# A fused recurrence, gated MLP and expert layer: TensorE's order planned with its instruction supply, one more group inverted in 32x32 blocks, an untaken branch moved to GpSimd, rows stored in four parts

## The chip, the cores and the metric

The kernel runs on one core of one Trainium2 chip. The metric is device microseconds of one launch. The kernel before took 984.58 us (median of 3 runs, 982.29 to 986.92).

## What is computed

Three stages follow one another, cut here to their core:

```python
# 1. a recurrence over S=768 steps, for B=4 batches and H=8 heads, state 40x40
y[t]  = r[t] @ state
Sa    = state @ a[t]
state = state * w[t] - outer(Sa, b[t]) + outer(v[t], k[t])
# 2. a gated MLP on x = y with the heads side by side (320 columns)
h = relu(x @ w_in); u, v = h[:, :512], h[:, 512:]
x = (u * (w_spatial @ layernorm(v) + b_spatial)) @ w_out
# 3. eight experts: a row goes to its argmax expert, or keeps the expert of the row
#    before it (a sequential choice along the 768 rows of a batch)
out = p[e] * (relu(x @ w1[e]) @ w2[e])
```

## The kernel before, in words

**Attention** (`attention`, from L158; 0 to 474 us) turns the recurrence into chunks of 64 steps. There are 12 chunks for each of 4 batches, 48 in all, numbered q = 0 to 47 with the batches interleaved; each handles all 8 heads as 4 pairs in the two halves of the partitions. Inside a chunk the steps depend on each other through a 64x64 triangular matrix per head, which has to be inverted. The chunks are inverted in seven groups (q 0 to 3, then 4 to 11, 12 to 19, 20 to 27, 28 to 35, 36 to 43, 44 to 47). A letter per group in `KEYS['inv']` (L57) says how. "b": VectorE inverts the 32x32 diagonal blocks by 31 pairs of a product and a subtraction (`prod` L321, `diff` L324), and TensorE joins two blocks to 64x64 (`c1` L391, `c2` L399). "c": VectorE inverts 16x16 blocks by 15 shorter pairs (`prod16` L332, `diff16` L335), and TensorE joins them first to 32x32, with two more sets of tiny products for every two chunks (`gA` L366, `pA` L376 and L379) and a VectorE correction between them (`gAc` L368). An fp32 product of these is two passes, and every pass is a weight load and a matmul, so that `pA` for two chunks is 192 instructions. Before the change the letters are `ccbcbcb`: four groups of 16x16, three of 32x32.

Per chunk there is also preparation: decay products by scans (`stF` L258, L262), scalings of k, b and a (`stK` L268, `stB` L273, on VectorE or GpSimd as the planner finds them free), their products (`stQ` L280, `stT` L298) and copies and masks on ScalarE and GpSimd. Then comes the chain of the chunk itself: `s`, `z`, `w`, `t`, `y` on TensorE (L434, L443 with L415, L452 and L453, L462, L470 and L471), with a copy or product on ScalarE or VectorE behind each (L436, L446, L456, L465 and L466, L476 and L478).

The order of all of this is not written by hand: `plan` (L58) simulates the engines on the host from a duration per operation (the numbers in the `add(...)` calls from L510 on), priorities computed from `KEYS`, and dependencies, and gives the list in which the instructions are issued. When TensorE has nothing ready, `fill` (L96) puts in dummy matmuls (`heat` L229, `tied` L239), which are there to keep TensorE's clock up. The planner keeps its own count of how busy TensorE has been (`cols`, `hw`, `th`, `hp`) and slows TensorE's durations when that is low. Loading and checking of the decays (`guard`) and some weight preparation of the MLP are fitted in among it, at priorities `gp` and `pp`.

**The branch.** The chunked form needs decays in a range; `guard` counts those outside. Behind attention all engines load the flag and branch (L1522, L1523) over `general` (L626), a loop of 12 times 64 steps with nine VectorE instructions a step. With these inputs it is never entered.

**The middle** (`middle`; to about 700 us) is the MLP; TensorE goes on there with `vprod` (L874), whose first operands VectorE splits at the end of attention (L816).

**The tail** (`tail`, to 754 us) finishes the last batch: output products (`outp`, copied to `xr` by L967 and L968), the gate's logits, the routing (`Q["begin"]` to `Q["enter"]`, mostly tiny VectorE operations: `begin` L1058 to L1075, `probs` L1078 to L1081, `rows` L1088 to L1091, `back` L1098 to L1100, `places` and `pick` L1105 to L1123, `enter` L1126), the storing of the rows for the experts' gathers (`store` L1130, on SP's queue), the slot tables (`slots`, `first`, `slots2`, L1135 to L1211), and for the first expert's weights, loaded by `prefetch` in five pieces, the split into two fp32r halves: `split` (L1237) casts a piece on ScalarE (L1240) and subtracts on VectorE or GpSimd (L1241, L1242). Before:

```python
Q["rows"](0); G.outp(0, xr); G.logits(LG, 1, ident, M.lt)
M.split(0, 0, G.nc.gpsimd)
Q["begin"](1); G.outp(1, xr); R["enter"](1); Q["rows"](1)
M.split(0, 1, G.nc.gpsimd)
G.outp(2, xr); Q["back"](); G.outp(3, xr, mid=Q["places"]); Q["probs"]()
M.store(b, xr, 0, 4); G.outp(4, xr); G.outp(5, xr, mid=lambda: Q["enter"](0))
M.store(b, xr, 4, 6); Q["enter"](1)
M.slots(); M.first(); M.split(0, 2); M.slots2()
```

**The experts** (`experts`, to the end) gather rows from the store (L1257), turn them (L1266, L1269, L1270) and multiply (L1279); pieces 3 and 4 of the first weights are split there on GpSimd.

## Time and profile before

| | us |
|---|---|
| runs, median (lowest to highest) | 984.58 (982.29 to 986.92) |
| the profiled execution | 995.05 |
| its span, first to last instruction | 993.5 |
| TensorE busy (matmuls) | 928.7 (93%) |
| VectorE busy | 687.4 (69%) |
| ScalarE busy | 549.8 (55%) |
| GpSimd busy | 385.2 (39%) |

Times in the rows are microseconds from the start of the span. PE is TensorE's matmuls, PEld its weight loads (beside them), DVE is VectorE, ACT ScalarE, POOL GpSimd, SP the engine whose queue issues most transfers; a "q" behind an engine is its queue, which handles branches and semaphores. Matmuls overlap, and their ends are modelled, so a busy PE isn't PE at its peak. PEclk is the granted share of TensorE's full clock (1.00 is 2.4 GHz, 0.50 is 1.2 GHz). An arrow names what ended an idle time; "issue" means that the profile shows nothing for which the engine waited.

### The profile page before, as it was taken

Reading aid. Unit: us, or ns where it says so; the run is one execution under the profiler, and the core shown is the slowest. Engines: PE = TensorE matmul, PEld = TensorE weight load, DVE = VectorE, ACT = ScalarE, POOL = GpSimd, SP = SyncE. Lnnn points to the kernel's source line nnn. Section 1 sums busy time; section 2 is a strip of 40 time slices with the busy share of each in tenths; the row PEclk is TensorE's granted clock in tenths of the full one; section 3 lists DMA queues with packets and bytes.
Section 4 is the critical chain, followed back from the end, with each engine's and each line's share of the span. In section 5 each row is a group of like instructions: output and inputs, shape, how many; then the busy total and the mean of one; then the engine's idle time right before and its main releaser. Section 6 shows DMA issues by size and latency. Waiting matters only on the chain. (4 is left out here: it accounts for less than half of the span.)

```text
span 993.5 us, 33733 instructions
## 1 busy us (share of the span) xinstructions
PE 928.7 (93%) x14053; PEld 820.3 (83%) x14053; DVE 687.4 (69%) x1614; ACT 549.8 (55%) x1251; POOL 385.2 (39%) x560
## 2 busy tenths in 40 slices
PE   8879989999899998899899999999999999999995
PEld 6657767787787776787789999999878999999994
DVE  6666779888669888764676464654675777787782
ACT  7766543766546774466344433434343767667671
POOL 6544733745216541452243025050136443333431
PEclk9687997999869999679899999999999999999998
DMA  6665761757615865245320030210147656444640
GB/s 160 169 165 136 166 154 50 190 127 187 164 45 128 214 156 113 67 113 131 112 61 1 10 89 1 56 42 1 50 166 270 257 209 248 167 161 160 266 158 16
DMA packets 172415, 127.52 MB, mean 128 GB/s; under 512 B 127502, under 2 KB 161168, under 8 KB 170593
## 3 DMA queue, kind: packets, MB, share of 16 engines
q1 hardware_dynamic: 166704, 78.06, 30.9%
q0 software_dynamic: 5552, 47.25, 12.6%
q8 instruction: 112, 1.84, 0.8%
q14 instruction: 47, 0.38, 0.1%
HBM read 108.13 MB, written 26.61 MB: 136 GB/s over the span
## 5 line engine op out<-in xcount | busy, mean ns | idle before, releaser
L1242 DVE TENSOR_TENSOR eWL<-raw,eWH 128x1024 fp32r<-128x1024 f32 (+1 forms) x64 | 86.2, 1356 | 21.2 <-ACT eWH L1240 19.9
L1240 ACT CAST eWH<-raw 128x1024 fp32r<-128x1024 f32 (+1 forms) x85 | 94.4, 1140 | 2.2 <-DMA raw<-in_wt_dram,wid 2.2
L1369 POOL DMA_INDIRECT out_dram<-yo,sid x29 | 39.2, 1352 | 111.7 <-ACT yo L1368 44.9
L229 PEld LDWEIGHTS <-hz 128*128 128x128 bf16 x607 | 56.9, 106 | 27.7 <-issue 11.8
L1279 PE MATMUL e_ph<-xh,eWH 128*128 128x256 f32 x288 | 77.9, 284 | 0.0
L294 POOL TENSOR_SCALAR_AFFINE_SELECT lq<-lq 64x256 f32<-64x256 f32 x96 | 47.0, 489 | 78.1 <-ACT lq L290 70.0
L1279 PE MATMUL e_ph<-xl,eWH 128*128 128x256 f32 x288 | 77.0, 280 | 0.0
L1279 PE MATMUL e_py<-eWH,hh 128*128 128x320 f32 x232 | 73.0, 315 | 0.0
L1279 PE MATMUL e_py<-eWH,hl 128*128 128x320 f32 x232 | 72.3, 312 | 0.2 <-DVE hl L1352 0.2
L1279 PE MATMUL e_py<-eWL,hh 128*128 128x320 f32 x232 | 71.5, 308 | 0.0
L936 PE MATMUL pv<-sh,g_vh 128*128 128x384 f32 x192 | 66.4, 346 | 1.3 <-ACT pv L926 1.2
L936 PE MATMUL pv<-sh,g_vl 128*128 128x384 f32 x192 | 64.9, 338 | 1.1 <-POOL g_vl L916 0.6
L273 POOL TENSOR_TENSOR lq<-etile,GP 64x256 f32<-64x256 f32 (+1 forms) x60 | 46.8, 780 | 46.3 <-DVE GP L262 28.5
L936 PE MATMUL pv<-sl,g_vh 128*128 128x384 f32 x192 | 64.6, 336 | 0.0
L426 POOL TENSOR_SCALAR_AFFINE_SELECT X<-X 64x256 f32<-64x256 f32 x48 | 23.2, 483 | 97.3 <-ACT X L422 81.2
L1326 DVE SCALAR_TENSOR_TENSOR hl<-e_ph,hh 128x256 fp32r<-128x256 f32 x96 | 37.9, 418 | 26.3 <-ACT hh L1325 23.3
L470 PE MATMUL py<-X,kt 128*40 128x104 f32 x384 | 51.4, 269 | 4.6 <-DVE X L465 4.3
L465 DVE TENSOR_TENSOR X<-pw,ut 64x416 f32<-64x416 f32 x48 | 27.8, 578 | 40.4 <-PE pw L462 28.8
L1279 PEld LDWEIGHTS e_ph<-xh,eWH 128*128 128x128 f32 x288 | 54.4, 189 | 0.9 <-ACT xh L1269 0.2
L1279 PEld LDWEIGHTS e_ph<-xl,eWH 128*128 128x128 f32 x288 | 54.3, 188 | 0.1
L1325 ACT ACTIVATE hh<-e_ph 128x256 fp32r<-128x256 f32 x96 | 36.5, 384 | 31.0 <-PE e_ph L1279 25.9
L1279 PE MATMUL e_ph<-xh,eWL 128*128 128x256 f32 x192 | 53.6, 279 | 0.0
(363 smaller groups left out, 3159.8 us busy)
## 6 DMA issues: line engine op xcount, KB each, us to landing
etile<-in_ed_dram SPq DMA_DIRECT2D x96, 161.2 KB
DT<-in_dd_dram SPq DMA_DIRECT2D x96, 80.0 KB
pu<-BP SPq DMA_DIRECT2D x48, 128.0 KB
yT<-yt SPq DMA_DIRECT2D x48, 104.0 KB
X<-in_vd_dram SPq DMA_DIRECT2D x96, 50.0 KB
groom<-in_w_dram SPq DMA_DIRECT2D x20, 192.0 KB
xs<-xr SPq DMA_DIRECT2D x3, 1176.0 KB
praw<-in_win_dram SPq DMA_DIRECT2D x6, 512.0 KB
```

The source lines that it names most:

```text
L229: nc.tensor.matmul(out=hcur[bank],lhsT=hz[:,0:128],rhs=hz,start=True,stop=True)
L273: eng.tensor_tensor(out=LQ[q][r,sl],in0=ar[r],in1=GP[q%NBIG][r,:,0:64],op=ALU.mult)
L294: nc.gpsimd.affine_select(out=LQ[q][r,h],in_=LQ[q][r,h],pattern=[[0,NP],[1,64]],**sel)
L465: nc.vector.tensor_tensor(out=x[0:64,:,0,:],in0=pw[0:64],in1=ut[0:64].unsqueeze(1).to_broadcast([64,NP,104]),op=ALU.mult)
L470: nc.tensor.matmul(out=py[0:40,p,:],lhsT=KT[q][:,p,0:40],rhs=x[:,p,0,:],start=False,**acc)
L936: for j,(l,r) in enumerate(t): nc.tensor.matmul(out=pv,lhsT=l,rhs=r,start=False,stop=j==len(t)-1,skip_group_check=True)
L1240: nc.scalar.copy(WH[:,c0:c1],raw[:,c0:c1])
L1242: else: V.tensor_tensor(out=WL[:,lc(c0):lc(c1)],in0=raw[:,c0:c1],in1=WH[:,c0:c1].bitcast(F32),op=ALU.subtract)
L1279: for i,(l,r) in enumerate(t): nc.tensor.matmul(out=out,lhsT=l,rhs=r,start=i==0,stop=i==len(t)-1)
L1325: nc.scalar.activation(hh[:,j],ph,AF.Relu)
L1326: V.scalar_tensor_tensor(out=hl[:,j],in0=ph,scalar=0.0,in1=hh[:,j].bitcast(F32),op0=ALU.max,op1=ALU.subtract)
L1369: nc.gpsimd.indirect_dma_start(out=out,out_offset=IO(ap=self.sid[:,h,s:s+1],axis=0),in_=yo[:,h],in_offset=None,bounds_check=B*S-1,oob_is_e ...
```

## The change

`inv` becomes `ccbcbbb`: group 5 (q 36 to 43) is inverted in 32x32 blocks. The planner gets a model of TensorE's instruction supply: it counts the instructions of each operation (`INS`), lets pages of 256 arrive `fl` = 6.1 us after they are asked for, holds TensorE when there are none, and adds `df` to the priority of an operation that would run dry. Its count of TensorE's activity is on a new scale (`cols`, `hw`, `th`, `hp`), several durations and priorities are new, and the guard's work gets an earlier place (`gp`). `general` computes on GpSimd instead of VectorE, its reductions as trees of additions. In `split` the weight tiles are made by the piece that comes first. In the tail the first two weight splits move, the probabilities come earlier, and the rows are stored in four parts instead of two.

```diff
-KEYS={'pp': 54.454, 'pj': 0.015, 'inv': 'ccbcbcb', 'nbp': 16, 'hold': 1.383, 'hp1': 0.062, 'b0': 4, 'nbig': 20, 'gp': 23.525, 'h0': 9.0, 'mM': 4, 'fF': -0.034, 'dv0': 8.889, 'nx': 4, 'na32': 2, 'nkb': 2, 'nab': 4, 'ne': 3, 'hw': 4600, 'ht': 1, 'hp': 8, 'th': 2950, 'hend': 1000000000.0, 'i0': 0.005, 'i1': -0.244, 'a1': -166.776, 'r1': 0.834, 'p1': -2.404, 'd1': -0.39, 'cA': 16.708, 'rA': 0.747, 'le': 1.448, 'qd': 48, 'dv': 18.251, 'ld': 1.673, 'vr': 0.758, 'c1': 2.004, 'cT': 11.353, 'dT': 6.376, 'dl': 0.9, 'xh': None, 'w': 0.04, 'tk': -0.5, 'gj': 1.2, 'gv': 1.0, 't0': 1.5, 'tl': 1.484}
+KEYS={'gj': 1.2, 'gv': 1.0, 't0': 1.796, 'tl': 0.585, 'pp': 54.454, 'pj': 0, 'inv': 'ccbcbbb', 'nbp': 16, 'hold': 1.383, 'hp1': 0.062, 'b0': 4, 'nbig': 20, 'gp': 11.797, 'h0': 9.0, 'mM': 4, 'fF': -0.034, 'dv0': 12.386, 'nx': 4, 'na32': 2, 'nkb': 2, 'nab': 4, 'ne': 3, 'hw': 8000, 'hf': 0, 'fl': 6.1, 'df': 2.857, 'ht': 1, 'hp': 20, 'th': 4800, 'hend': 1000000000.0, 'i0': 0.005, 'i1': -0.244, 'a1': -132.699, 'r1': 0.834, 'p1': -2.404, 'd1': -0.39, 'cA': 16.708, 'rA': 0.857, 'le': 1.448, 'qd': 48, 'dv': 18.251, 'ld': 1.673, 'vr': -0.099, 'c1': 2.004, 'cT': 11.353, 'dT': 6.376, 'dl': 0.9, 'xh': None, 'w': 0.04, 'tk': -0.5}
...
+    ic=0.; av=[]; nav=0; FL=K["fl"]
+    INS=dict(stQ=66,stT=17,vr=33,s=33,z=66,c1=65,c2=65,gA=129,pA=193,iZ=3,w=33,t=33,y=34,heat=2,tied=7)
...
-                return min(m)[2] if m else None
+                def cost(x):
+                    d=ops[x[2]][0][P]; lim=448+256*(nav+sum(v<=now+d for v in av[nav:]))
+                    return x[0]+K["df"]*(ic+INS.get(x[2][0],0)>lim),x[1]
+                return min(m,key=cost)[2] if m else None
...
+        ci=INS.get(run[P][0][0],0)/max(run[P][1],1e-6) if run[P] else 0.
+        while nav<len(av) and av[nav]<=now+1e-9: nav+=1
+        if ci and ic>=448+256*nav-1e-6: rate[P]=1e-9
...
+                ic+=dt*rate[e]*ci
+                while ic>=64+256*len(av)-1e-5: av.append(t+FL)
...
-    out=plan(ops,K,lambda n: SSQ[n[1]]>1,dict(stQ=512,stT=677,vr=324,s=320,z=860,c1=512,c2=512,gA=256,pA=768,iZ=160,w=1644,t=845,y=1700),takes,gives)
+    out=plan(ops,K,lambda n: SSQ[n[1]]>1,dict(stQ=1925,stT=1456,vr=963,s=602,z=2527,c1=1064,c2=1064,gA=1064,pA=2662,iZ=310,w=3328,t=1564,y=3328),takes,gives)
...
-    nc=tc.nc; V=nc.vector
+    nc=tc.nc; V=nc.gpsimd
...
+    def rows(o):
+        add(tm[:,0:5],tm[:,0:5],tm[:,5:10])
+        add(tm[:,0:2],tm[:,0:2],tm[:,2:4])
+        add(tm[:,0],tm[:,0],tm[:,1])
+        add(o,tm[:,0],tm[:,4])
+    def cols(o):
+        for n in (20,10,5): add(tm[:,:,0:n],tm[:,:,0:n],tm[:,:,n:2*n])
+        add(tm[:,:,0:2],tm[:,:,0:2],tm[:,:,2:4])
+        add(tm[:,:,0],tm[:,:,0],tm[:,:,1])
+        add(o,tm[:,:,0],tm[:,:,4])
...
-        if i==0: self.W[s]=[self.wps[s%2].tile([128,n],F32R,name=m,bufs=1) for m,n in (("eWH",WC),("eWL",WC-FF))]
+        if s not in self.W: self.W[s]=[self.wps[s%2].tile([128,n],F32R,name=m,bufs=1) for m,n in (("eWH",WC),("eWL",WC-FF))]
...
-    M.split(0, 0, G.nc.gpsimd)
     Q["begin"](1)
+    Q["probs"]()
     G.outp(1, xr)
     R["enter"](1)
     Q["rows"](1)
-    M.split(0, 1, G.nc.gpsimd)
+    M.store(b, xr, 0, 2)
     G.outp(2, xr)
     Q["back"]()
     G.outp(3, xr, mid=Q["places"])
-    Q["probs"]()
-    M.store(b, xr, 0, 4)
+    M.store(b, xr, 2, 4)
     G.outp(4, xr)
+    M.store(b, xr, 4, 5)
     G.outp(5, xr, mid=lambda: Q["enter"](0))
-    M.store(b, xr, 4, 6)
+    M.store(b, xr, 5, 6)
     Q["enter"](1)
+    M.split(0, 1, G.nc.gpsimd)
     M.slots()
     M.first()
     M.split(0, 2)
     M.slots2()
+    M.split(0, 0)
```

## Rows read from the trace of the kernel before

**Rows 1.** Stretches: bounds, length, each engine's busy time (count), PEclk, DMA share, GB/s.
```profile
149.60:163.30 13.70, 13.70 (x270) 11.10 (x261) 12.70 (x32) 4.97 (x14) 1.20 (x3) 0.50 0.08 21
265.70:293.00 27.30, 27.06 (x594) 23.56 (x595) 13.48 (x34) 11.99 (x33) 3.60 (x8) 0.50 0.18 46
293.00:316.00 23.00, 22.27 (x626) 18.49 (x625) 21.79 (x56) 12.09 (x29) 12.65 (x21) 1.00 0.43 113
316.00:361.00 45.00, 43.73 (x1186) 36.41 (x1181) 38.72 (x94) 34.05 (x88) 22.62 (x43) 1.00 0.73 179
361.00:398.80 37.80, 31.94 (x937) 26.21 (x935) 29.32 (x73) 18.63 (x48) 10.56 (x16) 1.00 0.62 129
398.80:412.50 13.70, 13.70 (x289) 11.82 (x287) 8.03 (x21) 6.54 (x17) 3.77 (x6) 0.50 0.17 42
412.50:432.90 20.40, 18.12 (x499) 16.03 (x497) 15.89 (x36) 10.59 (x23) 8.52 (x9) 0.67 0.44 111
478.80:484.10 5.30, 5.30 (x13) 4.14 (x14) 1.03 (x3) 0.60 (x1) 0.45 (x2) 0.50 0.66 198
...
484.10:700.00 215.90, 213.56 (x1232) 200.90 (x1231) 130.07 (x379) 93.79 (x216) 62.07 (x124) 1.00 0.13 35
```

**Rows 2.** Waits of TensorE, 85 to 475 us: total, times, longest.
```profile
PE pc L376 <- issue: 7.2, 5, 2.6
PE py L470 <- DVE X L465: 4.3, 4, 2.0
```

**Rows 3.** TensorE's timeline at the longest gap: start, length, instruction, idle before.
```profile
265.94 0.27 PE L376 MATMUL pc<-XT,GA 32*32 32x32 f32 x3 [2.60 <-issue]
```

**Rows 4.** TensorE's instruction queue, 246 to 268 us: packets, MB, share of 16 engines.
```profile
q8 instruction: 6, 0.10, 1.7%
```

**Rows 5.** Queue instructions of the branch line: count, duration, first and last start.
```profile
L1523 POOLq COMPARE_BRANCH  x1: 53/53/53, 463.8 to 463.8; - x1
...
L1523 DVEq COMPARE_BRANCH  x1: 72/72/72, 474.7 to 474.7; - x1
...
L1523 DVEq EVENT_SEMAPHORE  x1: 21/21/21, 478.7 to 478.7; - x1
```

**Rows 6.** Timeline behind the branch.
```profile
478.79 0.80 PE L874 MATMUL pv<-wh,X32y 128*128 128x512 f32 x1 [3.02 <-DVEq L1523]
...
479.01 0.10 POOL L828 MEMSET mh<- 128x1 f32 x1 [15.26 <-DVEq L1523]
```

**Rows 7.** TensorE's groups by line, 380 to 435 us: busy, mean ns, idle before.
```profile
L376 PE MATMUL pc<-XT,GA 32*32 32x32 f32 x256 | 5.5, 205 | 2.6 <-issue 2.6
L379 PE MATMUL pc<-GA,XT 32*32 32x16 f32 x128 | 5.2, 183 | 0.0
...
L366 PE MATMUL pc<-T,BP 32*32 32x16 f32 x256 | 3.6, 195 | 0.0
```

**Rows 8.** VectorE's groups by line, 0 to 475 us.
```profile
L321 DVE TENSOR_TENSOR pr<-A,X 128x31 f32<-128x31 f32 (+23 forms) x93 | 35.9, 386 | 2.5
L324 DVE TENSOR_TENSOR X<-X,pr 128x31 f32<-128x31 f32 (+23 forms) x93 | 35.8, 385 | 2.4
...
L368 DVE SCALAR_TENSOR_TENSOR GA<-pc,mk,I 128x128 f32<-128x128 f32 x14 | 4.9, 350 | 21.0 <-PE pc L366 20.8
```

**Rows 9.** VectorE's groups by line, 326 to 366 us (group 5's inversion).
```profile
L332 DVE TENSOR_TENSOR pr<-A,X 128x30 f32<-128x30 f32 (+7 forms) x15 | 4.5, 299 | 0.4
L335 DVE TENSOR_TENSOR X<-X,pr 128x30 f32<-128x30 f32 (+7 forms) x15 | 4.0, 268 | 0.4
```

**Rows 10.** Timeline of the tail, four instructions.
```profile
728.40 2.38 POOL L1242 TENSOR_TENSOR eWL<-raw,eWH 128x1024 fp32r<-128x1024 f32 x1 [6.57 <-DMA raw<-in_wt_dram]
728.45 2.37 DVE L1064 SCALAR_TENSOR_TENSOR cd<-dl,i8m 128x24 f32<-128x24 f32 x1
...
731.36 0.33 PE L1088 MATMUL pu<-idb,ab 128*1 128x128 bf16 x3 [1.28 <-DVE ab L1070]
...
746.46 1.38 POOL L1257 DMA_INDIRECT xg<-xs,gid  x1 [6.02 <-DVE wid L1198]
```

**Rows 11.** GpSimd's queue on the gathers' line: count, duration, first and last start.
```profile
L1257 POOLq EVENT_SEMAPHORE  x11: 17/17/43, 745.5 to 946.2; - x11
```

More of the change, by code (lines that the diff above doesn't have):

```diff
@@ L95, in pick, with heavy @@
             return n
+    def heavy(t): return sum(x[1] for x in recent if x[0]>=t-TK)
     def fill():
@@ L104, in fill @@
         if ties and ties[0][0]<=now:
-            plain=0; recent.append((now,512)); return ("tied",bk,ties.pop(0)[1])
+            plain=0; recent.append((now,540)); return ("tied",bk,ties.pop(0)[1])
         if plain<K["hp"] or now<K["h0"]:
-            plain+=1; recent.append((now,256)); return ("heat",bk)
+            plain+=1; recent.append((now,497)); return ("heat",bk)
     while left or any(x for x in run.values()):
@@ L113, in plan @@
             if run[e] or free[e]>now+1e-9: continue
-            n=pick(e)
+            n=pick(e) if e!=P or now<K["h0"] or heavy(now)>=K["hf"] else fill()
+            if n is None and e==P: n=pick(e)
+            if n is not None and n[0] in ("heat","tied"):
+                out.append((now,len(out),n,e)); run[e]=[n,.107 if n[0]=="heat" else .25,0.,[],False]
+                continue
             if n is None:
@@ L139, in plan @@
             elif free[e]>now+1e-9: nxt.append(free[e])
+        if ci and rate[P]<1e-6: nxt=[x for x in nxt if x<now+1e5]+av[nav:nav+1]
+        elif ci: nxt+=[now+(x-ic)/ci/rate[P] for x in (64+256*len(av),448+256*nav) if x>ic+1e-6]
         if run[P]: nxt.append((int(now/TK+1e-9)+1)*TK)
@@ L512, in attention @@
         add(("stB",q),al,a,stB,(q,),[E("stF",q),E("w",q-NBIG)])
-        add(("stQ",q),{P:.66},a,stQ,(q,),[E("stK",q),E("stB",q),E("stL",q-1),E("stLk",q-1),E("vrc",q-1) if 0 else None])
+        add(("stQ",q),{P:0.65},a,stQ,(q,),[E("stK",q),E("stB",q),E("stL",q-1),E("stLk",q-1),E("vrc",q-1) if 0 else None])
         add(("stL",q),{A:.37},a,stL,(q,),[E("stQ",q),("c1",(q-NBP)//2*2) if q>=NBP else None])
@@ L638, in general, with add @@
     sel=pool.tile([128,32],F32,name="s_sel")
-    V.tensor_reduce(out=sel,in_=ident.rearrange("p (g j) -> p j g",g=4),axis=AX.X,op=ALU.add)
+    def add(o,x,y): V.tensor_tensor(out=o,in0=x,in1=y,op=ALU.add)
+    add(sel,ident[:,0:32],ident[:,32:64])
+    for g in (2,3): add(sel,sel,ident[:,32*g:32*g+32])
+    def rows(o):
[8 more added lines that the diff above has]
+        add(o,tm[:,:,0],tm[:,:,4])
     V.memset(st,0.0)
@@ L651, in general @@
             V.tensor_tensor(out=tm,in0=st,in1=d("r"),op=ALU.mult)
-            V.tensor_reduce(out=yp[:,t],in_=tm.rearrange("p d e -> p e d"),axis=AX.X,op=ALU.add)
+            rows(yp[:,t])
             V.tensor_tensor(out=tm,in0=st,in1=e("a"),op=ALU.mult)
-            V.tensor_reduce(out=sa[:,:,0],in_=tm,axis=AX.X,op=ALU.add)
+            cols(sa[:,:,0])
             V.tensor_tensor(out=st,in0=st,in1=e("w"),op=ALU.mult)
```

32 lines of the change are left out of this document (16 added, 16 removed).

## The prediction, made before the changed kernel was run

> **What bounds the kernel now.** I read the busy shares first, then the stretches of the attention stage, then what ended TensorE's waits in it, then the two seams of the program (the branch behind attention, the tail ahead of the experts). The middle keeps TensorE at work for 213.56 of the 215.9 us from 484 to 700 at full clock [rows 1], and the change edits neither it nor the expert loop, so everything is decided before 484 us and in the tail (722 to 754 us). In attention TensorE is nominally busy nearly all the time, but in several stretches it runs at half its clock (1.2 GHz): 149.6 to 163.3, 265.7 to 293.0, 398.8 to 412.5, and a third of 412.5 to 432.9 is lost as well [rows 1]. VectorE is the second bound: 21.79 of 23.0 us (95%) in 293 to 316, 86% in 316 to 361 [rows 1].
>
> What precedes the half-clock stretches is a gap in TensorE's stream. The longest waits named "issue" (no semaphore, no engine) fall on one line, the products that join two 16x16 inverses (L376): 7.2 us in five gaps [rows 2]. The longest, 2.60 us, lies in the middle of such a burst, and it is there, at 265.7, that the clock falls [rows 1, 3]. In the 22 us round that gap the queue that carries TensorE's own instructions moved six packets, 0.10 MB, about 17 KB each [rows 4]: instructions come from memory in pages, and a burst of tiny matmuls eats them faster than they come. So some gaps look like want of instructions, and each is paid again in clock.
>
> At the end of attention VectorE takes the branch over the general recurrence: it compares at 474.7 and shows its next queue instruction at 478.7 [rows 5]. TensorE, with two products of the middle done, stands 3.02 us for that instruction, and then runs at half clock until 484.1 [rows 1, 6].
>
> **The branch.** The body that is jumped over holds 9 VectorE instructions times 64 steps; the change issues them, split into more, on GpSimd, so VectorE jumps over a few dozen. GpSimd's jump will be the long one: it compares at 463.8 and has nothing to do until 479.0, idle for 15.26 us [rows 5, 6], so 4 us there are hidden. Saved: 3.0 us of wait, plus half of the 5.3 us at half clock, 2.65 us. I take -5.0, since VectorE's last split must still end; ends 0 (another engine's jump takes its place) and -5.65.
>
> **Group 5 as 32x32.** This drops four times gA and pA. On TensorE these are 256 matmuls on L366, 256 on L376 and 128 on L379: 3.6 us, and 5.5 and 5.2 us that run interleaved, so about 9.0 us, and a gap of 2.6 us inside them [rows 7]. The half-clock stretch from 398.8 follows such a gap; half of its 13.7 us is 6.8 [rows 1]. TensorE's side: -18.4 us. VectorE's side: the three groups that already invert 32x32 cost 35.9 + 35.8 us, 23.9 us each [rows 8]; group 5 now costs 4.5 + 4.0 = 8.5 [rows 9], and its four correction instructions (0.35 each) fall away, 1.4 [rows 8]. So +14.0 us on VectorE, in 316 to 432.9, where it now works 92.0 of 116.9 us [rows 1]. With 106.0 us of work that stretch can't be shorter than 106.0 (gain 10.9); at the 95% of the best stretch it takes 111.6 (gain 5.3). I take -8: GpSimd, 45.5 us busy there [rows 1], can take some scaling from VectorE. Ends: -18.4 (VectorE hidden) and +6.3 (only the 86% of 316 to 361: 123.2 us).
>
> **The planned order.** The planner now counts TensorE's instructions, charges an operation that would run dry (df), and rescales its account of what keeps the clock up (hw, th, hp, the column table); priorities and durations move. What can be won outside group 5: the other L376 gaps, 7.2 - 2.6 = 4.6 us [rows 2, 7], and half-clock time. In 149.6 to 163.3 VectorE works 12.70 of 13.7 us, so a faster TensorE wins little there. In 265.7 to 293.0 VectorE works 13.48 of 27.3, and TensorE does 594 matmuls where the next stretch at full clock does 626 in 23.0: 594 would take 21.8 us, 5.5 less [rows 1]. Together -10.1. Not all bursts can be spread, so I take -8. Nothing in the trace shows the new order, so the ends are wide: -25 (all of 13.7 + 27.3 us at half clock won back, 20.5, and the 4.6), and +13.7 (one new stretch as long as the 27.3 us one, half of it lost). More fill matmuls and the guard's earlier loads cost nothing as long as they stand in idle time; ScalarE, busy for 12.09 of 23.0 us in 293 to 316, has room for the guard's share [rows 1]. If that cover fails, the guard delays the copies that free PSUM banks, inside the same ends.
>
> **The tail.** Taking the first weight split off GpSimd frees VectorE's routing: a comparison of 24 elements took 2.37 us, beginning 0.05 us after GpSimd's subtraction and ending with it, and TensorE then stood 1.28 us for its result [rows 10]. That is -1.3 on the way to the last one-hot products. The four probability operations move into a place where VectorE waits for TensorE: nothing. The rows now go out in four stores; SP issues two more, on a queue whose prefetch is over. Before, the first gather started at 746.46, 0.9 us after GpSimd passed its wait for the last store (745.5) [rows 10, 11]; a last store of 128 rows instead of 256 behind 512 lands earlier, perhaps 2 us. Against it: the moved split puts a ScalarE cast in front of the copy of the slot table, and its subtraction on GpSimd now runs beside the slot arithmetic, which has comparisons of the kind that stood 2.2 us; behind it in GpSimd's queue stands the gather. The first split comes last on VectorE, in front of the first expert's operand splits, which TensorE waits for. I take -0.7; ends -3.3 and +2.2.
>
> **Sum.** -5.0 - 8 - 8 - 0.7 = -21.7 us. The profiled execution took 995.05 us (span 993.5, the rest around it), 10.5 above the median of 984.58; it becomes 973.4, and the median 962.9. I say **963 us**.
>
> **A rule against the change.** The trace has a 2.60 us gap named "issue" inside a run of L376 matmuls [rows 3], and six instruction packets in 22 us [rows 4]. The Trainium skill, "Runtime: NRT & Kernel Launch", section Instruction fetch mechanics, says that straight-line fetch streams ahead by itself and is hidden because dispatch is slower than the fill; by it a planner that counts instructions counts nothing real, the planning term is 0, and the sum is -13.7. The trace speaks against that rule here, since nothing else is named for the gap, but it can't exclude it.
>
> **Rivals.** (1) The gaps are not want of instructions, and the new order is just another order: branch, group 5 and tail alone, 984.6 - 13.7 = 970.9. For it: the profile infers "issue" from absence. Against: the gaps sit on the densest bursts.
>
> (2) VectorE becomes the bound from 316 to 433 and takes what TensorE gives back: the stretch takes 116.9 us as before (VectorE at 91%), the order gives nothing, branch and tail remain: 984.6 - 5.7 = 978.9. For it: +14.0 us on an engine at 79% there.
>
> (3) The other side: in that stretch VectorE manages only 86%, group 5 costs +6.3, and TensorE, waiting for VectorE's product, loses its clock more often. It already stood 4.3 us in four waits for L465 [rows 2]. Two more stretches of 13.7 us at half clock cost 13.7. With branch and tail: 984.6 + 6.3 + 13.7 - 5.7 = 998.9. It decides from the point where the stretch takes over 122.6 us (116.9 + 5.7).
>
> (4) The order keeps TensorE fed and clocked nearly throughout: -18.4 - 20 - 5.7 gives 940.5.
>
> **How the numbers follow.** Forecast 0.50 (950 to 975), rival 1 0.14, rival 2 0.12, rival 3 0.14, rival 4 0.10. A measurement of this kernel tells about 0.5%, 4.9 us, from no change. Faster by more: 0.48 of the forecast, 0.12 of rival 1, 0.05 of rival 2, 0.10 of rival 4: 0.75. Within it: 0.02 + 0.02 + 0.05 + 0.02 = 0.11, the last from the near edge of rival 3. Slower: 0.02 of rival 2 and 0.12 of rival 3, 0.14. The range leaves out most of rival 3 above and the lower half of rival 4: 943 to 987 us. The forecast's own range is 950 to 975.
>
> **What would show it.** Branch: VectorE's compare and next queue instruction under 1 us apart, the wait of TensorE on it gone, clock full from 475 on. Group 5: 640 fewer matmuls on L366, L376 and L379 together, L321 and L324 at 124 each instead of 93, VectorE over 85% busy in the chunks 24 to 40. Order: fewer "issue" gaps on L376, less half-clock time between 85 us and the end of attention. Tail: the 24-element comparison back to a fraction of a microsecond, the gather sooner. The prediction is wrong if attention ends later than 474 us, or if it ends sooner by much more than the 16 us I give it.

## The result, and the profile after

The changed kernel took 995.37 us (median of 20 runs, 987.55 to 1007.86), the kernel before 988.61 us (median of 20, 981.06 to 996.50) in the same sessions. The ratio is 1.0072, with a 95% interval of 1.0045 to 1.0099: slower, by about 7 us, where the prediction said 22 us faster. All ratios here leave out, on either side, the executions more than 1.5% above the fastest of their kernel; where that decides a reading, the medians of all executions stand beside it. The profiled execution took 999.62 us (span 998.1).

Line numbers of the changed kernel are 17 higher in attention and 29 higher in the tail and the experts than those of before. First the stretches; the columns are those of [rows 1]. This is all of attention, to its last product, before:

```profile
0.00:474.00 474.00, 432.62 (x10823) 353.94 (x10824) 353.59 (x857) 286.74 (x746) 213.21 (x348) 0.89 0.57 138
```

and in the changed kernel, with two stretches of it:

```profile
0.00:476.30 476.30, 418.49 (x9930) 348.47 (x9931) 364.81 (x873) 284.83 (x734) 226.45 (x358) 0.83 0.55 136
...
335.00:357.60 22.60, 18.51 (x309) 15.74 (x310) 11.50 (x29) 10.37 (x27) 3.79 (x8) 0.62 0.27 69
...
316.00:433.00 117.00, 102.72 (x2352) 86.16 (x2349) 96.50 (x231) 64.32 (x161) 44.65 (x65) 0.91 0.48 117
```

Read the first pair as an account of TensorE; it is an estimate, which takes all work to slow down with the clock. A mean clock of 0.83 over 476.3 us means that 0.17 x 476.3 = 81 us' worth of full clock were lost; before it was 0.11 x 474.0 = 52. Its work, counted at full clock, fell from 432.6 - 52 = 380.5 to 418.5 - 81 = 337.5 us: 43 us less, most of it dummy matmuls (403 of their weight loads on one line instead of 607) and the joins of group 5. The loss to the clock rose by 29 us, the idle time from 41.4 to 57.8, by 16. Less work, and all of it given back: attention ends 2.3 us later.

Where the clock was lost says more. The first 316 us, before and changed:

```profile
0.00:316.00 316.00, 287.56 (x7014) 232.08 (x7015) 237.50 (x591) 189.16 (x507) 151.43 (x257) 0.88 0.57 142
```

```profile
0.00:316.00 316.00, 278.26 (x6856) 230.82 (x6858) 242.50 (x591) 194.72 (x519) 164.37 (x274) 0.79 0.59 146
```

By the same count 66 us' worth are lost here instead of 38, nearly all of the 29, and yet the changed kernel has chunk 24 done 1.0 us sooner (315.2 instead of 316.2 us). It falls behind in the last 8 chunks.

What TensorE waited for from 85 to 475 us (total, times, longest) [rows 2]:

```profile
PE py L487 <- DVE X L482: 8.7, 10, 3.0
PE pw L469 <- issue: 4.7, 3, 4.1
...
PE pc L393 <- issue: 1.0, 1, 1.0
```

The gaps on the joining products (L376, now L393) have shrunk from 7.2 to 1.0 us, as planned. The wait for VectorE's product, 4.3 us before, is 8.7. That is one row; all rows that name VectorE add up to 28.6 us instead of 10.0, and all that name "issue" to 10.5 instead of 12.6. So the 16 us more of idle time are waits for VectorE, though some of them may have lain before under the dummy matmuls that are gone. There is also a new "issue" gap of 4.1 us. It ends at 339.0, and the clock stands at half from 339.1 to 356.1, in the 22.6 us stretch shown above (0.62).

The branch, its queue instructions and the first product behind it [rows 5, 6]:

```profile
L1554 POOLq COMPARE_BRANCH  x1: 53/53/53, 466.4 to 466.4; - x1
...
L1554 DVEq COMPARE_BRANCH  x1: 72/72/72, 477.1 to 477.1; - x1
...
L1554 DVEq EVENT_SEMAPHORE  x1: 21/21/21, 478.6 to 478.6; - x1
```

```profile
478.36 0.47 PE L903 MATMUL pv<-wh,A32x 128*128 128x512 f32 x1 [0.30 <-PEq L1554]
```

VectorE's jump takes 1.5 us instead of 4.0, TensorE's 3.02 us wait is gone, and the clock no longer falls behind it. GpSimd's own jump grows from 0.4 us (463.8 to 464.2) to 3.7 (466.4 to 470.1), hidden in its idle time.

The tail, first TensorE's longest wait in it, then the timeline of VectorE and GpSimd [rows 10]:

```profile
PE e_ph L1308 <- DVE xl L1299: 6.6, 1, 6.6
```

```profile
726.03 0.18 DVE L1093 SCALAR_TENSOR_TENSOR cd<-dl,i8m 128x24 f32<-128x24 f32 x1
...
738.10 2.35 DVE L1198 TENSOR_TENSOR dc<-cc 128x16 f32<-128x16 f32 x1
...
741.44 2.04 POOL L1286 DMA_INDIRECT xg<-xs,gid  x1 [1.02 <-DVE gid L1170]
...
745.71 6.48 DVE L1235 TENSOR_SCALAR se<-vs,pidx 128x20 f32<-128x20 f32 x1
...
746.41 5.73 POOL L1271 TENSOR_TENSOR eWL<-raw,eWH 128x1280 fp32r<-128x1280 f32 x2
...
752.76 1.22 DVE L1271 TENSOR_TENSOR eWL<-raw,eWH 128x1024 fp32r<-128x1024 f32 x1
753.90 1.01 DVE L1299 TENSOR_TENSOR xl<-e_px,xh 128x384 fp32r<-128x384 f32 x2
```

Two forecasts came true: `cd` takes 0.18 us instead of 2.37, and the first gather starts sooner. In the trace it is 5.0 us (741.44 instead of 746.46), but that holds the branch's gain and attention's 2.3 us; with the tail alone (experiment 1) the gather starts 270.0 us behind the end of attention instead of 272.5, 2.5 us sooner. But then GpSimd, done with its gathers sooner, begins its two subtractions (weight pieces 3 and 4) while VectorE still has the slot table to finish. A comparison of 20 numbers, 0.30 us before, ends with GpSimd's second subtraction, after 6.48 us. Behind it stand the last weight split and then `xl`, for which TensorE waits 6.6 us; then it runs at half clock from 752.1 to 762.3 (before: from 750.4 to 753.8). The 61st of the experts' products begins 4.4 us later than before, though the first began 5.4 us sooner. The Trainium skill, "SBUF — State Buffer", section Who interferes with whom, says that VectorE and GpSimd share a pair of ports and that, where an instruction of each needs it, whoever issues first gets it for the whole instruction and the other fully blocks. The trace agrees on the blocking (6.48 us instead of 0.30) and shows two things more. VectorE's instruction stood for two GpSimd instructions in a row. And its record begins 0.70 us ahead of the first of them, when GpSimd was at an indirect load (745.36 to 746.38); what held it in that time is not shown.

So the reading to be tested is: the branch gives its 5 us, the tail costs 7, and the order gains nothing, perhaps by single waits such as the 4.1 us before 339.0.

### The profile page after: what moved, and what is told of

It reads as the page before. It is cut to its first block, busy times and chain, and to the rows that moved or that the text cites. A ratio compares the mean times of both kernels' runs of the same rounds, so it can differ in the third digit from the quotient of the medians.

```text
span 998.1 us, 31999 instructions
## 1 busy us (share of the span) xinstructions
PE 914.5 (92%) x13169; PEld 816.0 (82%) x13169; DVE 706.9 (71%) x1633; ACT 548.6 (55%) x1239; POOL 391.0 (39%) x569
## 3 DMA queue, kind: packets, MB, share of 16 engines
q0 software_dynamic: 5552, 47.25, 12.6%
## 5 line engine op out<-in xcount | busy, mean ns | idle before, releaser
L1398 POOL DMA_INDIRECT out_dram<-yo,sid x29 | 34.7, 1198 | 115.4 <-ACT yo L1397 57.0
L487 PE MATMUL py<-X,kt 128*40 128x104 f32 x384 | 56.3, 284 | 9.0 <-DVE X L482 8.7
L460 PE MATMUL py<-DT,SD 40*40 40x104 f32 (+1 forms) x768 | 56.0, 285 | 5.6 <-DVE yt L495 3.7
L469 PE MATMUL pw<-X,lq 128*64 128x104 f32 x384 | 54.4, 294 | 4.7 <-issue 4.7
L246 PEld LDWEIGHTS <-hz 128*128 128x128 bf16 x403 | 37.5, 105 | 23.6 <-issue 13.9
```

The lines of the kernel that those rows point to most:

```text
L246: nc.tensor.matmul(out=hcur[bank],lhsT=hz[:,0:128],rhs=hz,start=True,stop=True)
L460: nc.tensor.matmul(out=PY[q][r:r+m,p,:],lhsT=SD[q%2][r:r+40,p,0:m],rhs=DT[q%3][r:r+40,p,64:168],start=p==0,**acc)
L469: nc.tensor.matmul(out=pw[0:64,p,:],lhsT=LQ[q][:,0,p,:],rhs=x[:,p,0,:],start=True,stop=True)
L487: nc.tensor.matmul(out=py[0:40,p,:],lhsT=KT[q][:,p,0:40],rhs=x[:,p,0,:],start=False,**acc)
```

## Experiment 1: the parts, one at a time

Each is the kernel before with one part of the change, word for word: the general recurrence on GpSimd; the tail (and `split`); `KEYS`, `plan` and the durations; and that last with one letter taken back.

> The kernel before with only the general recurrence on GpSimd. Theory A (the three parts of the change add up; the profiled executions differ by +3.3 us at the first product behind attention, by -5.7 at the first gate product behind the branch, by +6.9 in the tail): about -5.7 us, ratio 0.994, TensorE's 3.02 us wait for VectorE's branch gone and the clock full behind it. Rival B (another engine's jump takes its place): 0, ratio 1.000.

> The kernel before with only the new tail (splits moved, probabilities earlier, four stores). Theory A: the loss of the tail belongs to the tail's own edits. The gathers come about 4 us sooner, GpSimd begins its two weight splits while VectorE still has the slot table to finish, and VectorE's comparison (se) stands for the whole of them: TensorE waits 6 to 7 us for xl: +7 us, ratio 1.007. Rival B: the collision comes only from the shifted times behind the new attention, and the tail alone is -0.7 to -2 us, ratio 0.998.

> The kernel before with only the new order of attention and group 5 in 32x32 blocks. Theory A: attention ends 2 to 3 us later, ratio 1.003, with over 150 us at half clock before its end (before: 106). Rival B: the order is where the whole loss is, +7 us, ratio 1.007. The prediction on record said -16 us, 0.984.

```diff
-'inv': 'ccbcbbb'
+'inv': 'ccbcbcb'
```

> The same new order, but group 5 inverted in 16x16 blocks as before (the planner plans again). Theory A (VectorE takes what TensorE gives back: in the changed kernel VectorE is busy for 38.1 of 40 us in 361 to 401 and 30.5 of 33 in 401 to 434): the same time as the new order with group 5 in 32x32 blocks, within 4 us. Rival B (group 5 is worth the 8 us of the prediction and the order alone loses 10): 8 us slower than that, ratio near 1.011.

| part | median us | ratio (95% interval) | about us |
|---|---|---|---|
| branch | 984.76 | 0.9971 (0.9922 to 1.0020) | -2.9 |
| tail | 992.87 | 1.0074 (1.0023 to 1.0124) | +7.3 |
| order, group 5 in 32x32 | 993.69 | 1.0047 (1.0002 to 1.0092) | +4.6 |
| order, group 5 in 16x16 | 1002.42 | 1.0135 (1.0085 to 1.0184) | +13.3 |

The first three add up to +9.0 us, the whole change to +7.1 (1.0072): theory A holds within the intervals, and the loss is the tail's and the order's. The branch's time leaves its theory A and its rival B both open; its trace has TensorE's wait gone and full clock behind it. In the run of the tail alone, TensorE's wait and VectorE's comparison are there as in the changed kernel, without the new attention in front:

```profile
PE e_ph L1279 <- DVE xl L1270: 6.6, 1, 6.6
```

```profile
738.93 6.46 DVE L1206 TENSOR_SCALAR se<-vs,pidx 128x20 f32<-128x20 f32 x1
```

The fourth row speaks against its theory A, for its rival B: under the new planner group 5 is worth 8.7 us (1.0135 to 1.0047), what the prediction said, and the order without it loses 13.

One more thing is seen here. Attention of before, the same instructions in the same order, ended at 474.0 us in the profile that the prediction used, at 465.4 in the run of the branch and at 464.7 in that of the tail. Mean clocks to the end were 0.89, 0.91 and 0.90. The profile that was read was a long one.

## Experiment 2: is it the clock?

Theory C: the planner's new account takes TensorE for busy enough and leaves dummy matmuls out, so the clock falls. Three kernels try it from both sides, and a fourth takes the supply model out of the planner.

```diff
-'hw': 8000
+'hw': 1000000000.0
```

> The new order alone (no branch, no tail edits) with one number changed: the planner's limit on its account of TensorE's activity (hw) is lifted, so that every idle moment of the plan gets dummy matmuls; 888 of their weight loads are issued instead of 472 (before: 716). Theory C (the new order loses because its new account takes TensorE for busy enough and leaves out dummy matmuls: 80 to 235 us holds 67 of them in the changed kernel, 268 before, and the clock falls there): the half-clock time before the end of attention comes down from 171 to about 110 us, ratio 0.985 to 0.992, against 1.0047 with the limit. Rival D (more dummies use up the instruction supply, or the order itself is bad): gaps named issue grow, ratio stays at 1.000 to 1.010.

```diff
-'fl': 6.1, 'df': 2.857
+'fl': 0.0, 'df': 0.0
```

> The new order alone, with the supply model taken out of the planner (pages arrive at once, no penalty for an operation that would run dry); it plans 813 dummy weight loads. Theory C: as with the limit lifted, 0.985 to 0.995, because the dummies are back. Rival E (the supply model is what is right in the new planner): without it the gaps on the lines that join 16x16 inverses come back (7 us before, 2 us in the new order) and the time is worse than 1.0047.

The same order, with dummies where the plan leaves TensorE idle:

```diff
                 n=fill() if e==P else None
-                if n is None: continue
+                if n is None:
+                    bk=min(bank,key=bank.get)
+                    if e==P and bank[bk]+.25<=now and now>=ghost+.1:
+                        ghost=now; out.append((now,len(out),("heat",bk),e))
+                    continue
```

> The new order alone, every engine's instructions in the very same order, with 246 dummy matmuls added where the plan leaves TensorE idle (718 weight loads of dummies, as many as the 716 before). Theory C' (it is the missing dummies: the same order of before, run four times, ended attention at 465.4 us with 82 us at half clock and at 474.0 with 106, 0.36 us for a us): half-clock time from 171 to about 110 us, 15 to 20 us less, ratio 0.985 to 0.990. Rival G (the order is held up by VectorE and ScalarE; where they hold it, a TensorE at half clock is no later): the half-clock time falls but the ratio stays at 1.000 to 1.010.

The order of before, with dummies taken out:

```diff
         for t_,_,n,e in out:
+            if n[0] in ("heat","tied") and 80<t_<235:
+                some+=1
+                if some%4: continue
```

> The kernel before with its own order, with three of four dummy insertions left out that its plan has between 80 and 235 us (531 weight loads of dummies instead of 716). Theory C' (the clock needs them and the time needs the clock): half-clock time up by 40 us or more in 80 to 235, ratio 1.012 to 1.025. Rival G: TensorE saves the dummies' own time and waits for the others anyway, ratio 0.997 to 1.004.

Measured: limit lifted 1.0219 (1.0181 to 1.0258); no supply model 1.0261 (1.0216 to 1.0306); dummies added to the same order 1.0017 (0.9971 to 1.0062); dummies taken out of the order of before 1.0182 (1.0112 to 1.0252). The stretch from 80 to 235 us (columns as above) in the kernel before and with its dummies thinned:

```profile
80.00:235.00 155.00, 145.81 (x3849) 119.18 (x3842) 127.90 (x311) 92.11 (x241) 80.25 (x135) 0.93 0.59 145
```

```profile
80.00:235.00 155.00, 136.28 (x3467) 112.20 (x3464) 121.22 (x297) 87.24 (x227) 78.12 (x130) 0.79 0.55 137
```

In the order of before the dummies are worth 18 us: without three quarters of them the clock falls from 0.93 to 0.79, TensorE does 382 fewer matmuls in the stretch (181 of them the dummies themselves), VectorE falls behind with it, and attention ends at 487.2. That is theory C', for that order.

For the new order it is not borne out. Dummies added to the very same order raised the mean clock of the whole execution from 0.913 to 0.9285 (medians of 12 executions each; before: 0.947), some 15 us' worth of full clock, and the time fell by 3 us, less than the intervals can tell. The profile of that run is one of its slowest executions (998.49 us) and shows no more clock to the end of attention than without dummies (0.82), so the test stays inconclusive. With the limit lifted the kernel was slower than theory C and rival D had it; without the supply model it was worse than 1.0047, as rival E had it. All of attention with the supply model taken out:

```profile
0.00:472.80 472.80, 419.14 (x10272) 342.20 (x10273) 364.89 (x880) 283.98 (x734) 220.85 (x352) 0.94 0.56 137
```

In this profile the clock is better (0.94) than in any profile of the order of before (0.89 to 0.92), and attention is no sooner than in most of them (472.8; 464.7 to 474.0). It is the fastest of its six executions, though: its clock over the whole execution is 0.959, those of the other five 0.927 to 0.956, and the kernel before had 0.948 in the same session (median). With the limit lifted it is 0.935 in the profiled execution and 0.918 to 0.932 in the others. So part of the 6 to 10 us by which the medians of these runs exceed their profiles (998.3 and 998.5 us) may be clock. Against the new order as it was (0.913, ratio 1.0047) both have more clock and are 17 and 21 us slower: more granted clock did not make these orders fast.

What the supply model counts can be read from the traces. TensorE's own instruction queue over the whole kernel before:

```profile
q8 instruction: 112, 1.84, 0.8%
```

That is 112 packets of 16,384 bytes for 28,436 recorded instructions of TensorE (weight loads, products and those of its sequencer), 254 a packet. Numbered from the start, each of its 13 "issue" gaps of at least 0.5 us between 60 and 476 us stands in front of an instruction whose number is 193 or 194 above a multiple of 256, and each ends 1.2 to 1.5 us after a packet has landed. In the 20 traces of this record 155 of 159 such gaps stand there, against 9 of 261 waits that name an engine or a load. The other four are one and the same wait, that of experiment 3, in four kernels. The planner's model holds TensorE at that place, too: in the diff, `448+256*nav` is 192 above a multiple of 256. So these gaps are want of instructions. From 85 to 475 us they add up to 12.6 us before, 6.1 in the new order, and 11.9 in that order without the model, so the model halves them, and both signs of rival E are there. How much of the 21 us between the last two comes from that is not shown.

## Experiment 3: one instruction in ScalarE's queue

The wait that ends at 339.0 us is named "issue". ScalarE's timeline in the changed kernel shows what was late, and SP's when the load was issued:

```profile
337.75 0.67 ACT L725 ACTIVATE praw<-praw 128x512 f32<-128x512 uint32 x1 [5.21 <-DMA X<-in_vd_dram]
338.44 0.50 ACT L463 COPY X<-py 40x416 f32<-40x416 f32 x1
338.96 0.50 ACT L464 COPY X<-py 40x416 f32<-40x416 f32 x1
...
332.30 0.35 SPq L724 DMA_DIRECT2D praw<-in_win_dram  x1
```

The first conversion of the MLP's weights (`low`) stands in ScalarE's queue ahead of the copies of chunk 28 and waits 5.21 us for its 512 KB, issued at 332.30 (the last part landed at 337.59; the view names a smaller load behind it, which landed 0.16 us later). Behind it are the copies that TensorE's next products (L469) need, and ScalarE is idle meanwhile. The plan had it there because in the plan the load had landed. The test moves this one instruction back by five places on its queue, and changes nothing else; every other engine keeps its order.

```diff
+    i=next(j for j,x in enumerate(out) if x[2]==("wi",0,1,"low")); x=out.pop(i)
+    k=[j for j in range(i,len(out)) if out[j][3]==A][5]
+    out.insert(k,x)
```

> The new order alone, with one ScalarE instruction moved back by five places on its own queue: the first conversion of the MLP's weights, which stood for its load (2.55 us in the run of the new order, 5.21 us in the changed kernel) in front of the copies of chunk 28, after which TensorE had gaps of 1.8 and 4.08 us and 13.7 and 17.1 us at half clock. Theory H (this one instruction costs 6 to 8 us): ratio 0.997 to 1.000, chunk 28 under 10 us, no half clock at 339. Rival: another wait takes its place, 1.004 to 1.006.

Measured: 0.9956 (0.9915 to 0.9998) on the new order alone, against 1.0047 without the move: 9 us, give or take 6, where 6 to 8 were expected. Chunks 28 and 29 in the new order and with the move (the same 309 matmuls):

```profile
337.60:357.10 19.50, 17.08 (x309) 14.80 (x310) 11.73 (x30) 10.36 (x27) 3.82 (x8) 0.65 0.24 61
```

```profile
333.20:345.80 12.60, 11.47 (x309) 9.47 (x309) 11.47 (x30) 8.38 (x23) 3.56 (x7) 1.00 0.37 92
```

19.5 us become 12.6, 6.9 us less, and the clock stays full. The profiles differ by 11.6 us at the end of attention (476.2 and 464.6), but 4.4 of these lie ahead of the moved instruction, between equal orders. So the trace puts its price near 7 us. ScalarE's row has no wait any more:

```profile
334.75 0.68 ACT L716 ACTIVATE praw<-praw 128x512 f32<-128x512 uint32 x1
```

Theory H holds. "Issue" was here not a want of instructions, but a late engine that the view did not name.

## Experiment 4: what group 5 is worth

> The kernel before with the branch on GpSimd and group 5 in 32x32 blocks, planned by the planner of before with all its other numbers. Theory (group 5 is worth the 8 us of the prediction by itself; under the new planner it measured 1.0047 against 1.0135): ratio 0.985 to 0.990. Rival 2 of the prediction (VectorE takes what TensorE gives back): the branch alone, 0.997.

> The new order with group 5 in 16x16 blocks (1.0135), with the same ScalarE instruction moved back by five places; it stood 2.66 us for its load there too. Theory I (the 9 us between that order and the one in 32x32 blocks are the accident of this wait and its half clock, and group 5 is worth nothing, as under the old planner, 0.9974 against 0.9971): 0.994 to 1.002. Rival J (group 5 is worth 8 us, as predicted): 1.004 to 1.008, that is 8 to 12 us above the 0.9956 of the same repair with 32x32 blocks.

Under the old planner, with the branch moved: 0.9974 (0.9948 to 1.0000), the branch alone being 0.9971. Nothing. Chunks 28 to 39 with the branch alone, and with group 5 in 32x32 blocks as well:

```profile
334.10:422.70 88.60, 79.23 (x2243) 66.76 (x2239) 72.85 (x184) 51.93 (x127) 31.34 (x46) 0.92 0.52 127
```

```profile
334.20:418.10 83.90, 74.94 (x1811) 61.96 (x1805) 78.78 (x188) 49.12 (x122) 31.82 (x47) 1.00 0.50 124
```

These chunks gain 4.7 us, with VectorE at 78.78 of 83.9 us (94%), where the prediction took 95%. The last 8 chunks give it back. With the branch alone, and with both:

```profile
422.70:465.40 42.70, 39.23 (x986) 32.94 (x983) 25.39 (x49) 28.68 (x68) 16.12 (x20) 0.97 0.52 119
```

```profile
418.10:467.20 49.10, 42.55 (x874) 34.88 (x875) 33.90 (x70) 27.71 (x61) 19.24 (x21) 1.00 0.47 109
```

VectorE has 70 instructions there instead of 49: part of the last group's inversion and of the MLP's weights has been pushed behind, and the 8 chunks take 6.4 us more at full clock. In the changed kernel, too, the last 8 chunks take 48.8 us (VectorE 29.73, 64 instructions) where before they took 42.6 (25.57, 49); there the clock is down as well, 0.83 instead of 0.98.

Under the new planner, with the instruction moved in both: 1.0124 (1.0077 to 1.0172) in 16x16 blocks, 0.9956 in 32x32, so 16 us by the runs, above the 8 to 12 of rival J. Theory I falls: it is no accident of that wait. The profiles, 10.2 us apart at the end of attention, show where it lies. Chunks 28 to 39 in 16x16 and in 32x32 blocks:

```profile
333.70:433.40 99.70, 85.43 (x2252) 71.36 (x2253) 79.46 (x185) 54.69 (x132) 44.77 (x55) 0.84 0.53 122
```

```profile
332.10:413.20 81.10, 72.22 (x1745) 59.96 (x1744) 76.93 (x183) 46.98 (x117) 32.73 (x46) 1.00 0.49 118
```

Here 18.6 us are gained, and the last 8 chunks give 9.9 back (41.0 and 50.9 us). By the same marks, TensorE's last product of a chunk, the order of before with the branch moved takes 89.1 us for chunks 28 to 39 in 16x16 blocks. So what the new order loses without group 5 it loses in these twelve chunks, not ahead of them (332.7 us with the branch alone, 333.7 here). So group 5 is worth nothing in one order and 9 to 16 us in the other; in the second case the planner planned the whole order again, so that this is the worth of the letter and of what the plan made of it. The clock differs: 0.80 to the end of attention in the order with 16x16 blocks,

```profile
0.00:474.80 474.80, 429.55 (x10506) 359.06 (x10507) 354.08 (x845) 287.98 (x746) 225.74 (x360) 0.80 0.56 138
```

against 0.91 in the order of before [experiment 1]. That TensorE's work counts more where it runs at half clock fits this, but is argued, not shown.

## Experiment 5: the tail

The turn of the first gathered rows goes ahead of the two splits on GpSimd, whose casts stand in ScalarE's queue, so that GpSimd starts them after VectorE's table is done.

```diff
+                turn(lo)
                 for i in (3,4): self.split(0,i,nc.gpsimd)
-            turn(lo)
             if lo:
+                turn(lo)
                 prepare(lo)
```

> The kernel before with the new tail, and in the expert stage the first turn of the gathered rows issued ahead of the casts and subtractions of weight pieces 3 and 4. Theory A (GpSimd's two subtractions, begun early, hold up VectorE's comparison for 6.5 us in front of the operand split): VectorE's comparison is back under 0.5 us, TensorE's wait for xl under 2 us, ratio 0.994 to 0.998 against 1.0074 for the tail alone. Rival F (the first weight split, put last on VectorE, or the later stores are what costs): still above 1.003.

Measured on the kernel before with the new tail: 0.9953 (0.9917 to 0.9990), against 1.0074: 12 us from one line moved, give or take 6. In the traces the way from the end of attention to the 61st of the experts' products is 8.5 us shorter (286.1 instead of 294.6); to the 401st, behind the second gather, 5.0 are left (335.7 instead of 340.7; before the change 334.2). The comparison and GpSimd's subtractions now:

```profile
739.79 2.36 DVE L1169 TENSOR_TENSOR dc<-cc 128x16 f32<-128x16 f32 x1
...
747.41 0.24 DVE L1206 TENSOR_SCALAR se<-vs,pidx 128x20 f32<-128x20 f32 x1
...
750.90 5.87 POOL L1242 TENSOR_TENSOR eWL<-raw,eWH 128x1280 fp32r<-128x1280 f32 x2 [2.82 <-ACT eWH L1240]
```

Theory A holds, rival F falls. `dc` still stands 2.36 us beside GpSimd's split of piece 1, as the prediction feared for the slot arithmetic. The next kernel takes that split to VectorE and puts the branch in:

```diff
-    M.split(0, 1, G.nc.gpsimd)
     M.slots()
     M.first()
+    M.split(0, 1)
     M.split(0, 2)
```

> The kernel before with the branch on GpSimd and the new tail, the first turn ahead of the splits of pieces 3 and 4, and the split of piece 1 on VectorE behind the first gather's indices, so that no GpSimd subtraction runs beside VectorE's slot table (it held a 0.17 us operation for 2.36 us there). The parts add up: -2.9 us (branch), -4.6 (tail with the turn ahead), -2 (slot table): ratio 0.988 to 0.993. Rival: VectorE, with one split more, is the last in front of the operand split, and the tail gives what it gave with the turn ahead alone: 0.992 to 0.996.

Measured: 0.9956 (0.9921 to 0.9991), so the rival: no more than the tail with the turn ahead, without the branch. `dc` is back at 0.17 us and the turn comes 3.1 us sooner than in the run of the branch alone, but 2.5 us of it are lost again by 767: the second gather stands behind GpSimd's subtractions, and TensorE waits for its rows twice:

```profile
746.67 0.52 PE L1278 MATMUL e_px<-ident,xg 128*128 128x128 f32 x3 [1.17 <-DMA xg<-xs,gid]
747.97 0.52 PE L1278 MATMUL e_px<-ident,xg 128*128 128x128 f32 x3 [0.79 <-DMA xg<-xs,gid]
```

Two tries put pieces 3 and 4 on VectorE as well.

```diff
-                for i in (3,4): self.split(0,i,nc.gpsimd)
...
+                        if s==0 and j in (2,4): self.split(0,2+j//2)
```

> The kernel before with the branch on GpSimd and the new tail, in which no weight piece of the first expert is split on GpSimd any more: piece 1 on VectorE behind the first gather's indices, pieces 3 and 4 on VectorE behind the third and fifth product group of the first expert. Theory (with the turn ahead, the gain of 3 us in the tail was given back behind it, by a 2.75 us gap of TensorE at 745.2, because the second gather stands behind GpSimd's subtractions until 743.5): the second gather starts 3 us sooner, the gap is under 0.5 us, ratio 0.988 to 0.993 against 0.9956. Rival: VectorE's two splits delay the operands hl that TensorE waits for by as much, 0.994 to 0.997.

> The changed kernel with the one ScalarE instruction moved back (0.9956 for the order alone with that) and the same tail as the run without GpSimd splits. The parts add up: -4.4 us (order with the instruction moved), -2.9 (branch), -5 to -8 (tail): ratio 0.984 to 0.990. Rival: the parts overlap, 0.992 to 0.996.

Both were misses, 1.0109 (1.0052 to 1.0165) and 1.0104 (1.0047 to 1.0161): placed so, the splits stand behind the load of the third expert's weights into the same buffer. They wait for it (ScalarE's cast for 13.56 us), and the first expert's second product uses pieces 3 and 4 of the other expert's weights. The second try puts that load behind them:

```diff
                         if s==0 and j==0:
                             self.numbers(ps)
-                            ahead()
-                        if s==0 and j in (2,4): self.split(0,2+j//2)
+                            gather(1)
+                        if s==0 and j==1: self.split(0,3)
+                        if s==0 and j==3:
+                            self.split(0,4)
+                            gather(2)
+                            weights(2)
```

> The kernel before with the branch on GpSimd and the tail without GpSimd splits, in the order that keeps the first expert's weights apart from the third's: the second gather behind the first product group, pieces 3 and 4 on VectorE behind the second and fourth, and only then the load of the third expert's weights into the same buffer (in the run before this one that load was issued first, the splits waited for it and took its data: TensorE lost 11 us there). Theory: the second gather starts about 3 us sooner than behind GpSimd's subtractions, the 2.75 us gap of TensorE is gone: ratio 0.988 to 0.993 against 0.9956. Rival (VectorE's splits hold up hl, or the gather's rows come no sooner): 0.994 to 0.998.

> The changed kernel with the ScalarE instruction moved back and that same tail. Theory: -4.4 us (order with the instruction moved) on top of the run above, 0.984 to 0.990. Rival: the parts overlap as in the changed kernel with two repairs (0.9955): 0.992 to 0.997.

0.9991 (0.9959 to 1.0024) and 0.9977 (0.9929 to 1.0024); by the medians of all executions 981.55 and 983.64 us against 985.75. The waits for the second gather are gone from the trace, and yet the runs are not clearly faster than 0.9956: rivals. What is gained in one profile at this place, 1 to 3 us, is below what the runs can tell.

## Experiment 6: do the two waits account for the loss?

The changed kernel with two repairs only, the `low` instruction of experiment 3 and the turn of experiment 5.

> The changed kernel with two repairs only: the one ScalarE instruction moved back by five places, and the first turn ahead of GpSimd's subtractions of pieces 3 and 4. Theory (these two waits are what made the changed kernel slower; they measured -9 us on the new order and -12 us on the new tail): from 1.0072 to 0.985 to 0.992. Rival (the loss is spread over the order, and moving one instruction moved the noise): above 0.998.

Measured: 0.9955 (0.9908 to 1.0001), against 1.0072 without them, 11.5 us. By the medians of all executions it is 986.96 us against 985.48 for the kernel before, and the changed kernel's 995.37 against 988.61: 5 us. Either way the two waits account for the loss within the intervals, and this kernel can't be told from the one before. It is short of the 0.985 to 0.992 expected, since the gains do not add up: the parts gave -2.9, -4.4 and -4.6 us alone, -12 together, and the whole gives about -4.4. None of the kernels here is faster than the kernel before by more than 0.5%; the best (0.9953 to 0.9956) can't be told apart.

## Why the prediction was wrong

**The branch** (-5.0, ends 0 and -5.65) was right in its mechanism: GpSimd's jump lies in its idle time, TensorE's 3.02 us wait and the half clock behind it are gone. Timed alone it gave -2.9 us, with an interval that holds both 0 and -5; in its trace the way from the end of attention to the 61st of the experts' products is 5.0 us shorter.

**Group 5** (-8) was right in its terms. 640 matmuls went, VectorE's products rose to 124 of each kind, its work on the inversions rose by 15.3 us (112.5 to 127.8; forecast: 14.0), and under the old planner chunks 28 to 39 went at 94% of VectorE (experiment 4). In the changed kernel VectorE was busy for 96.50 of 117.0 us in 316 to 433, 82%, under the 85% that were to show it. What was left out is where the 14 us of VectorE's work go beyond that stretch: into the last 8 chunks, which the prediction took as given. Under the old planner that left nothing (rival 2), under the new one 9 to 16 us.

**The planned order** (-8, ends -25 and +13.7) is the step that failed. With group 5 left as it was, it measured +13.3 us, at the far end; counted the other way round, as what the order adds to group 5 under the old planner, it is some +5 (1.0047, where group 5 added nothing). The step took the gaps and half-clock stretches that the trace showed, and counted how many of them could go. The gaps did go (7.2 us on L376 became 1.0), but the half-clock time grew, and an order planned afresh brings waits of its own: those for VectorE rose from 10.0 to 28.6 us. The sentence that ScalarE, "busy for 12.09 of 23.0 us in 293 to 316, has room" costed a cover by an engine's busy share. In a queue that is issued in a fixed order, an instruction that waits for a load blocks all behind it whether the engine is busy or not: one ScalarE instruction, idle for 5.21 us, cost 7 us by the trace and 9 by the runs. It was not the guard's, which the prediction named, but the same kind. The rest of the order's loss without group 5 (1.0124 with that instruction moved) lies in chunks 28 to 39 (99.7 us instead of 89.1), at a clock of 0.84 instead of 0.92; what makes it is open: no run gave that order its clock back.

**The tail** (-0.7, ends -3.3 and +2.2) measured +7.3. The two gains were right: the tail alone brought the gather 2.5 us sooner (forecast: 1.3 for the freed routing and perhaps 2 for the smaller last store, the 2 worked out from no row; the runs don't part them). The collision of GpSimd's split with the slot arithmetic came as feared (2.35 us). What was missed is that a sooner gather also starts what stands behind it in GpSimd's queue. The prediction looked at the two splits that the diff moves and not at pieces 3 and 4, which it doesn't touch.

**The rule against the change**, by which planning for the instruction supply would be worth nothing, falls as far as the gaps go, and the first half of rival 1 with it: they stand at one place in every 256 instructions, and the model halves them (12.6 to 6.1 us, experiment 2). In time that was not enough to pay for the new order.

**Rival 3** came nearest (998.9 us; measured 995.37), by another way. TensorE did wait more for VectorE (10.0 to 28.6 us, on the product of L465 4.3 to 8.7) and lost more clock. But the stretch by which it decides went faster: from the end of chunk 24 to that of chunk 39 112.3 us instead of 115.2, and the clock lost ahead of it cost no time. With the 1.0 us won before that and the 6.2 us lost in the last 8 chunks this is the whole of attention's 2.3 us.

## What to carry to other kernels

An engine's idle time is cover only for work that is ready when its turn comes: for every instruction that a change moves ahead in a queue, look up when its input lands, and what stands behind it. When a step is made sooner, follow the queue that it stands in further, to the next thing that now starts sooner and to whom it meets there. And an order that is planned anew should be priced by how well the old plan foretold its own trace, not by the waits that it is meant to remove; no run here has tried that.

## What was not expected of the hardware

- A VectorE comparison of 128x20 numbers (0.24 to 0.30 us alone) took 6.46 to 6.48 us beside two GpSimd subtractions in a row; its record ended only when both had.
- The same program, its instructions in the same order, ended attention between 464.7 and 474.0 us in profiles of the kernel before and of kernels that share its attention, with mean clocks of 0.89 to 0.92.
- Taking out some 185 dummy weight loads with their matmuls, work that computes nothing, made the kernel 18 us slower (11 to 25).
- TensorE ran dry at one place in every 256 of its instructions: 155 of 159 gaps that no engine explains stand there, and in the kernel before each ended 1.2 to 1.5 us after a packet of 16,384 bytes on its instruction queue had landed.
- The other four are an engine that waits for a DMA two steps away: moving that engine's instruction removed the gap.
